# Two units at a time on the two row halves of the matrix array, in a two-MLP kernel on one core

## The chip, the cores and the metric

The kernel runs on one core of a Trainium2 chip. The metric is the device time of one execution in microseconds (us). TensorE (PE) multiplies matrices; VectorE (DVE), ScalarE (ACT) and GpSimd (POOL) work element by element; SyncE (SP) issues most of the transfers. A matmul multiplies a stationary operand (the weights, up to 128 rows by 128 columns) by a moving one (here 512 columns) and adds into one of eight PSUM banks, each of which holds 128 x 512 numbers in fp32. The rows of the array are the contraction dimension.

## The reference

```
x = softmax-weighted causal convolution of the input over 7 taps, 8 heads
                                     # [8192, 192]
h = x @ w_in1;   g = maximum(0.01*h, h);                      x = g @ w_out1
h = x @ w_in2;   g = h if h >= 1, 0 if h <= -1, else (h+1)^2/4;  out = g @ w_out2
                                     # w_in [192, 2048], w_out [2048, 192], all fp32
```

## The kernel before

The 8192 tokens are cut into 16 blocks of T = 512 (index j), the 2048 hidden channels into 16 slices of 128 (index f). One **unit** is (m, j, f): MLP m, block j, slice f. There are 512 of them. A unit has an up product (x of the block times one slice of w_in, into a bank h), a gate on ACT, DVE and POOL, and a down product (gate times one slice of w_out, added to the accumulators of the block).

To keep fp32 accuracy every operand is split in two numbers of type fp32r, a high part and a low part, and a product is high x high, high x low and low x high. x has 192 channels: 128 (part 0) and 64 (part 1). In part 1 the 64 channels lie twice in the 128 rows of the tile, and the weights `wi_b` hold the high part in one half and the low part in the other, so that all three products of part 1 take two matmuls. An up product is thus 3 + 2 = 5 matmuls of 128 rows x 512 columns (lines L584). The down product is 5 matmuls as well (L593): three for the output channels 0 to 127, and two for the channels 128 to 191, where `wo_b` holds high and low part side by side. So there are 10 matmuls to a unit and 5120 in all.

The gate of MLP 1 (m = 0) is two ACT activations (`gh`, and h itself) and one DVE subtraction (`gl`). The gate of MLP 2 (m = 1) is a DVE clamp (`s`), an ACT square, a DVE maximum (`g`), an ACT cast (`gh`) and a POOL subtraction (`gl`).

The order of all instructions comes from a planner (`Plan`) in the kernel: each step has an engine, a cost in ns and the steps that it depends on, and steps with a due time are put in order by how late they may be. The chip then runs each engine's list in that order. The first three blocks of MLP 1 run interleaved (`OFF`, `N0`), while the weights are loaded and split. After that units of MLP 1 and of MLP 2 alternate, and each MLP has two accumulator banks of its own (`acc_banks`): 4 and 5, and 6 and 7. The first three blocks also have their convolution done in part on PE (lines L529 and L534, plain fp32 matmuls, which need two passes); for the others DVE does all taps (L523).

Of the kernel before, what the change touches and what calls it, by code (L numbers as in the profile page):

```python
# [145 lines left out]
def kernel(  # L146
# [34 lines left out]
    PASS = 233  # L181
    UNIT = 10 * PASS
    LAG = 4

    HEAD = 0

    OFF = (0, 2, 4)
    N0 = len(OFF)

    E0 = 3  # L190

    CONV_BANKS = ((2, 3, 4), (5, 7, 6), (6, 7, 6))
# [4 lines left out]
    GO = 8  # L197
# [30 lines left out]
    wi_h = [cp.tile([128, NF, 128], F32R, name=f"wi_h{m}") for m in range(2)]  # L228
    wi_l = [cp.tile([128, NF, 128], F32R, name=f"wi_l{m}") for m in range(2)]
    wi_b = [cp.tile([128, NF, 128], F32R, name=f"wi_b{m}") for m in range(2)]  # L230
# [5 lines left out]
    def add_weights(t, m, o, g):  # L236
# [7 lines left out]
        def load():  # L244
# [7 lines left out]
            else:  # L252
                w = (w_in1, w_in2)[m].bitcast(U32)
                c = g * 512
                nc.sync.dma_start(out=t[:, 0:256].rearrange("p n t -> p (n t)"), in_=w[0:128, c:c + 512])  # L255
                for e in range(2):
                    nc.sync.dma_start(  # L257
                        out=t[DB * e:DB * (e + 1), 256:CW].rearrange("p n t -> p (n t)"),
                        in_=w[128:D, c + 256 * e:c + 256 * (e + 1)],
                    )  # L260
# [41 lines left out]
        if o == 0:  # L302
            part_a = lambda: ba()[:, 0:256].rearrange("p (k c) -> p k c", k=2)
            copy(400, wi_h[m][:, k, :], part_a)
            for e in range(2):
                r = slice(DB * e, DB * (e + 1))
                copy(300, wi_b[m][r, 2 * g + e], lambda r=r: ba()[r, 256:CW], 1)
            sub(pool, 930, wi_l[m][:, k, :], part_a, wi_h[m][:, k, :])
            for e in range(2):
                r = slice(DB * e, DB * (e + 1))  # L310
                q = slice(DB * (1 - e), DB * (2 - e))
                sub(pool, 450, wi_b[m][q, 2 * g + e], lambda r=r: ba()[r, 256:CW], wi_b[m][r, 2 * g + e], 1)
# [98 lines left out]
    xT, x1, x2 = {}, {}, {}  # L411

    spare = buf("x2", -4, [128, 4, T], F32R)
# [4 lines left out]
    def add_split(y, dst, part, lo_on=dve):  # L418

        hi, lo = 2 * part, 2 * part + 1  # L420
# [8 lines left out]

    def add_conv(at, j):  # L430
# [7 lines left out]
        dst = x1[j] = buf("x1" if j >= 2 else "x2", at, [128, 4, T], F32R)  # L438
# [98 lines left out]
        for i in range(2):  # L537
# [27 lines left out]
            add_split(y, dst, i, pool if (j, i) in LO_POOL else dve)  # L565


    acc = {}

    def add_unit(t, u):  # L570
        m, j, f = u
        src = (x1, x2)[m][j]
        h = bank(h_bank(t), t)
        a, b = buf("gh", t, [128, T], F32R), buf("gl", t, [128, T], F32R)
        first, last = f == 0, f == NF - 1
        if first:
            acc[m, j] = [bank(i, t) for i in acc_banks(m, j)]
        p = acc[m, j]

        def up(part):  # L580
            v = src()
            wh, wl, wb = wi_h[m][:, f], wi_l[m][:, f], wi_b[m][:, f]
            for i, (w, k) in enumerate(((wb, 2), (wb, 3)) if part else ((wh, 0), (wh, 1), (wl, 0))):
                nc.tensor.matmul(  # L584
                    out=h(), lhsT=w, rhs=v[:, k], start=(part == 0 and i == 0), stop=(part == 1 and i == 1)
                )

        def down(part):
            wh, wl = wo_h[m][:, f], wo_l[m][:, f]
            wb = wo_b[m][:, f].rearrange("p a d -> p (a d)")  # L590
            todo = ((wb, a), (wb, b)) if part else ((wh, a), (wl, a), (wh, b))
            for i, (w, v) in enumerate(todo):
                nc.tensor.matmul(  # L593
                    out=p[part](), lhsT=w, rhs=v(), start=(first and i == 0), stop=(last and i == len(todo) - 1)
                )

        key = ("w", m, 0, f // 2)
        for part in range(2):
            plan.add(
                pe, (2 if part else 3) * PASS, lambda part=part: up(part), reads=[(src, 2 * part), (src, 2 * part + 1), (key, part)],  # L600
                writes=[h, (h, part)] + (["under way"] if t == GO else []), uses=[src], due=UNIT * t - (HEAD if t == 0 else 0), chain=(h, "up"),
            )
        if m == 0:

            for dst in (a, h):
                plan.add(
                    act, 590,
                    lambda dst=dst: nc.scalar.activation(out=dst(), in_=h(), func=ACTF.Prelu, alpha=0.01),  # L608
                    reads=[h], writes=[dst], uses=[h],
                )  # L610
            plan.add(
                dve, 680, lambda: nc.vector.tensor_tensor(out=b(), in0=h(), in1=a(), op=ALU.subtract),  # L612
                reads=[h, a], writes=[b],
            )
        else:

            g, s = buf("g", t, [128, T]), buf("s", t, [128, T])
            plan.add(
                dve, 680, lambda: nc.vector.tensor_scalar(s(), h(), 1.0, -1.0, ALU.min, ALU.max),  # L619
                reads=[h], writes=[s],  # L620
            )
            plan.add(
# [185 lines left out]
```

## Time and profile before

| | |
|---|---|
| median of 3 executions | 1194.58 us (1194.23 to 1195.46) |
| span of the profiled execution, first to last instruction | 1192.7 us |
| busy in it: PE, PE weight load | 1186.8 us, 972.7 us |
| busy in it: DVE, ACT, POOL | 782.7 us, 734.3 us, 438.2 us |
| mean granted clock of PE, share of full speed | 0.999 |

The profile gives the span of the profiled execution; its own device time is not listed beside it, and the median of the three timed executions lies 1.9 us above the span. "Busy" of PE is the time in which at least one matmul is under way. Matmuls overlap, so that many more can fit into the same busy time; what counts is the time from the start of one to the start of the next.

### The profile page before, as it was taken

What the parts mean: (1) busy time and instruction counts of PE and PEld (TensorE: products, weight loads), DVE (VectorE), ACT (ScalarE), POOL (GpSimd) and SP (SyncE); (2) the same over time, 40 slices, a digit from 0 to 9 for tenths busy, and PEclk for the clock granted to TensorE, in tenths of its full rate; (3) what the DMA queues carried; (4) which work ended last, traced back from release to release, by engine and by line L of the source; (5) the groups of instructions that cost most, each with busy time, mean ns of one, the idle gap of its engine ahead of it and who ended that gap; (6) DMA issues with size and microseconds to landing.
All of it is one profiled execution on the core that took longest, in us unless ns stands there. A gap on an engine that the chain in (4) does not pass through costs nothing.

```text
span 1192.7 us, 15464 instructions
## 1 busy us (share of the span) xinstructions
PE 1186.8 (100%) x5210; PEld 972.7 (82%) x5210; DVE 782.7 (66%) x1209; ACT 734.3 (62%) x1296; POOL 438.2 (37%) x407
## 2 busy tenths in 40 slices
PE   9999999999999999999999999999999999999998
PEld 5788888888888888888888888888888888888887
DVE  7899897748567494764847658485674545447664
ACT  6777866656565565655656566565655656556654
POOL 4566374323223232232323233232233222335554
PEclk9999999999999999999999999999999999999999
DMA  4443111101001010010101001010000000000000
GB/s 132 117 104 99 43 43 18 23 1 23 10 9 23 1 23 9 15 18 1 32 1 23 10 10 23 1 23 1 1 14 1 14 1 3 12 1 14 14 14 14
DMA packets 114000, 27.90 MB, mean 23 GB/s; under 512 B 103680, under 2 KB 111872, under 8 KB 113920
## 3 DMA queue, kind: packets, MB, share of 16 engines
q1 hardware_dynamic: 113504, 26.69, 10.3%
q8 instruction: 40, 0.66, 0.2%
q14 instruction: 40, 0.33, 0.1%
q10 hardware_dynamic: 416, 0.23, 0.1%
HBM read 20.61 MB, written 6.29 MB: 23 GB/s over the span
## 4 chain that ended last, share of the span: by engine, by line
PE 99%; DMA 0%; SPq 0%; DVE 0%; issue 0%; ACT 0%; ACTq 0%
PE bank L584 49%; PE bank L593 49%; PE bank L529 1%; DMA wraw<-in_x_dram 0%; PE bank L534 0%; PE bank L328 0%; PE bank L478 0%; SPq L257 0%; PE bank L697 0%; SPq L255 0%; DVE s L714 0%; SPq L469 0%; DVE s L723 0%; ACT s L723 0%; ACTq L723 0%
## 5 line engine op out<-in xcount | busy, mean ns | idle before, releaser
L632 POOL TENSOR_TENSOR gl<-g,gh 128x512 fp32r<-128x512 f32 x256 | 343.2, 1343 | 677.6 <-ACT gh L630 674.7
L619 DVE TENSOR_SCALAR s<-bank 128x512 f32<-128x512 f32 x256 | 176.3, 689 | 303.4 <-PE bank L584 302.2
L584 PE MATMUL bank<-x,wi_h 128*128 128x512 f32 x1024 | 317.5, 391 | 0.0
L584 PE MATMUL bank<-x,wi_b 128*128 128x512 f32 x1024 | 316.9, 391 | 0.0
L623 ACT ACTIVATE s<-s,half 128x512 f32<-128x512 f32 x256 | 184.8, 722 | 192.7 <-DVE s L619 191.4
L630 ACT CAST gh<-g 128x512 fp32r<-128x512 f32 x256 | 158.6, 620 | 180.8 <-DVE g L627 178.1
L584 PEld LDWEIGHTS bank<-x,wi_h 128*128 128x128 f32 x1024 | 191.9, 188 | 42.2 <-issue 1.7
L584 PEld LDWEIGHTS bank<-x,wi_b 128*128 128x128 f32 x1024 | 192.2, 188 | 41.4 <-issue 1.4
L627 DVE TENSOR_TENSOR g<-bank,s 128x512 f32<-128x512 f32 x256 | 175.5, 686 | 67.8 <-ACT s L623 67.7
L593 PE MATMUL bank<-gh,wo_b 128*128 128x512 f32 x512 | 199.3, 389 | 0.0
L593 PE MATMUL bank<-gh,wo_h 128*128 128x512 f32 x512 | 199.3, 389 | 0.0
L593 PE MATMUL bank<-gl,wo_h 128*128 128x512 f32 x512 | 199.2, 389 | 0.0
L584 PE MATMUL bank<-x,wi_l 128*128 128x512 f32 x512 | 199.2, 389 | 0.0
L593 PE MATMUL bank<-gl,wo_b 128*128 128x512 f32 x512 | 199.2, 389 | 0.0
L593 PE MATMUL bank<-gh,wo_l 128*128 128x512 f32 x512 | 199.2, 389 | 0.0
L608 ACT ACTIVATE gh<-bank 128x512 fp32r<-128x512 f32 x256 | 152.8, 597 | 46.8 <-PE bank L593 25.3
L612 DVE TENSOR_TENSOR gl<-bank,gh 128x512 fp32r<-128x512 f32 x256 | 174.2, 680 | 9.8 <-ACT bank L608 9.2
L608 ACT ACTIVATE bank<-bank 128x512 f32<-128x512 f32 x256 | 151.8, 593 | 0.0
L523 DVE SCALAR_TENSOR_TENSOR xy<-xT,taps,xy 128x512 f32<-128x512 f32 x159 | 136.0, 878 | 0.2
L593 PEld LDWEIGHTS bank<-gl,wo_h 128*128 128x128 f32 x512 | 96.1, 188 | 20.0
L593 PEld LDWEIGHTS bank<-gh,wo_b 128*128 128x128 f32 x512 | 96.1, 188 | 20.0
L593 PEld LDWEIGHTS bank<-gh,wo_h 128*128 128x128 f32 x512 | 96.1, 188 | 20.0
(93 smaller groups left out, 741.5 us busy)
## 6 DMA issues: line engine op xcount, KB each, us to landing
xy<-in_x_dram SPq DMA_DIRECT2D x104, 64.0 KB, 2.4
wraw<-in_moe_w_out_dram SPq DMA_DIRECT2D x16, 384.0 KB, 3.0
out_dram<-o SPq DMA_DIRECT2D x90, 64.0 KB, 1.9
wraw<-in_moe_w_in_dram SPq DMA_DIRECT2D x16, 256.0 KB, 2.7
wraw<-in_moe_w_in_dram SPq DMA_DIRECT2D x32, 64.0 KB, 2.6
wraw<-in_x_dram SPq DMA_DIRECT2D x3, 384.0 KB, 5.3
out_dram<-s SPq DMA_DIRECT2D x1, 192.0 KB, 2.0
out_dram<-s ACTq DMA_DIRECT2D x1, 192.0 KB, 2.0
```

The costliest lines, as they stand in the source:

```text
L523: nc.vector.scalar_tensor_tensor(out=ys[i](), in0=t()[:, i, k:k + T], scalar=taps[:, i, k:k + 1], in1=ys[i](), op0=ALU.mult, op1=ALU.add,)
L529: nc.tensor.matmul(out=ys[1](), lhsT=flat(k), rhs=t()[:, 1, 2 * k:2 * k + T], start=(k == 0), stop=(k == NP - 1))
L584: nc.tensor.matmul(out=h(), lhsT=w, rhs=v[:, k], start=(part == 0 and i == 0), stop=(part == 1 and i == 1))
L593: nc.tensor.matmul(out=p[part](), lhsT=w, rhs=v(), start=(first and i == 0), stop=(last and i == len(todo) - 1))
L608: lambda dst=dst: nc.scalar.activation(out=dst(), in_=h(), func=ACTF.Prelu, alpha=0.01),
L612: dve, 680, lambda: nc.vector.tensor_tensor(out=b(), in0=h(), in1=a(), op=ALU.subtract),
L619: dve, 680, lambda: nc.vector.tensor_scalar(s(), h(), 1.0, -1.0, ALU.min, ALU.max),
L623: act, 720, lambda: nc.scalar.activation(out=s(), in_=s(), func=ACTF.Square, scale=0.5, bias=half),
L627: dve, 680, lambda: nc.vector.tensor_tensor(out=g(), in0=h(), in1=s(), op=ALU.max),
L630: plan.add(act, 620, lambda: nc.scalar.copy(a(), g()), reads=[g], writes=[a])
L632: pool, 1390, lambda: nc.gpsimd.tensor_tensor(out=b(), in0=g(), in1=a(), op=ALU.subtract),
```

## The change

Units are taken in **pairs** (m, j, p), slices 2p and 2p+1. In the up product the array is split into its upper and lower 64 rows. Slice 2p runs on rows 0 to 63 and slice 2p+1 on rows 64 to 127, each into a bank of its own. The 192 channels are three chunks of 64. The halves of x part 0 hold chunk 0 and chunk 1 (kept straight); a crossed copy of x holds chunk 1 and chunk 0 (made by DMA, or for the first block by ACT and DVE); part 1 holds chunk 2 twice. Each of the three steps has three products on both halves, so an up pair is 9 pairs of half-height matmuls. The weights of w_in are loaded in the layout that this needs, and `wi_b` is gone.

The down products of the first two blocks stay full height, 10 matmuls to a pair of units (L675 of the changed kernel). All later ones run on the halves too: each of the 10 matmuls becomes two with 64 rows, of which the lower half adds into a second set of accumulators. A chain of down products now owns four banks (4 to 7), and both MLPs share them, so one chain (m, j) runs at a time: all 8 pairs of a block, then the next block. At its end `gather` adds the two sets (an ACT copy and a DVE addition, twice). Two blocks instead of three are interleaved at the start. The order of PE's main products is now one fixed list (`steps`, chain "main"): the up product of pair n+2, then the down product of pair n.

```diff
-    OFF = (0, 2, 4)
-    E0 = 3
+    E0 = 2
-    COUNT = dict(wraw=4, wf=2, wa=2, wp=2, xy=4, xT=2, x1=2, x2=3, yz=2, g=2, s=2, gh=4, gl=4, o=1)
+    COUNT = dict(wraw=4, wf=2, wa=2, wp=2, xy=4, xT=2, x=3, yz=3, g=2, s=2, gh=4, gl=4, o=1)
...
+    def half_rows(outs, todo, start, stop):
+        for i, (w, v) in enumerate(todo):
+            for e, out_ in enumerate(outs):
+                r = slice(DB * e, DB * (e + 1))
+                nc.tensor.matmul(
+                    out=out_(), lhsT=w[e][r], rhs=v[e][r], start=start and i == 0, stop=stop and i == len(todo) - 1
+                )
...
+        def up(c):
+            v = src()
+            cols = [slice(128 * k, 128 * (k + 1)) for k in ((0, 1), (1, 0), (2, 2))[c]]
+            wh, wl = ([w[m][:, p, q] for q in cols] for w in (wi_h, wi_l))
+            hi, lo = ([v[:, 2 * c + i]] * 2 for i in range(2))
+            half_rows(hs, ((wh, hi), (wh, lo), (wl, hi)), c == 0, c == 1)
...
+            if full:
+                for i, (w, v) in enumerate(todo):
+                    nc.tensor.matmul(
+                        out=out_[part](), lhsT=w, rhs=v, start=start and i == 0, stop=stop and i == len(todo) - 1
+                    )
+            else:
+                half_rows(out_[part::2], [([w] * 2, [v] * 2) for w, v in todo], start, stop)
...
+    def gather(t, p, part):
+        z = buf("yz", t, [128, T])
+        plan.add(act, 590, lambda: nc.scalar.copy(z(), p[part]()), reads=[p[part]], writes=[z])
+        plan.add(
+            dve, 690, lambda: nc.vector.tensor_tensor(out=z(), in0=p[part + 2](), in1=z(), op=ALU.add),
+            reads=[p[part + 2], z], writes=[z],
+        )
+        return z
...
+    chains = [(0, 2), (1, 0), (1, 1)]
+    for j in range(3, NB):
+        chains += [(0, j), (1, j - 1)]
+    chains.append((1, NB - 1))
...
+    steps = ["U0", "U1", "D0"]
+    for n in range(2, EARLY, 2):
+        steps += [f"U{n}", f"U{n + 1}", f"D{n - 1}", f"D{n}"]
+    steps += [f"U{EARLY}", f"U{EARLY + 1}", f"D{EARLY - 1}"]
+    for n in range(EARLY, len(pairs)):
+        steps += [f"U{n + 2}"] * (n + 2 < len(pairs)) + [f"D{n}"]
```

On PE, in the middle of the program, one unit of MLP 2 stands so before (5 up matmuls, 5 down matmuls; `x2` means two with the same operands' names):

```order
L584 MATMUL bank1_65<-x2_3970,wi_h1_83 128x512 x2
L584 MATMUL bank1_65<-x2_3970,wi_l1_85 128x512
L584 MATMUL bank1_65<-x2_3970,wi_b1_87 128x512 x2
L593 MATMUL bank7_71<-gh_5235,wo_b1_93 128x512
L593 MATMUL bank7_71<-gl_5236,wo_b1_93 128x512
L593 MATMUL bank6_70<-gh_5235,wo_h1_89 128x512
L593 MATMUL bank6_70<-gh_5235,wo_l1_91 128x512
L593 MATMUL bank6_70<-gl_5236,wo_h1_89 128x512
```

In the changed kernel every row is a matmul on one half, and the rows come in twos. Here are the last two rows of an up pair and the first half of the down pair behind it, also in the middle of the program:

```order
L590 MATMUL bank0_64<-x_3561,wi_l0_84 128x512
L590 MATMUL bank1_65<-x_3561,wi_l0_84 128x512
L590 MATMUL bank5_69<-gh_4424,wo_b1_91 128x512
L590 MATMUL bank7_71<-gh_4424,wo_b1_91 128x512
L590 MATMUL bank5_69<-gl_4425,wo_b1_91 128x512
L590 MATMUL bank7_71<-gl_4425,wo_b1_91 128x512
L590 MATMUL bank4_68<-gh_4424,wo_h1_87 128x512
L590 MATMUL bank6_70<-gh_4424,wo_h1_87 128x512
L590 MATMUL bank4_68<-gh_4424,wo_l1_89 128x512
L590 MATMUL bank6_70<-gh_4424,wo_l1_89 128x512
L590 MATMUL bank4_68<-gl_4425,wo_h1_87 128x512
L590 MATMUL bank6_70<-gl_4425,wo_h1_87 128x512
```

So 10 rows of a down product take the place of 5, two by two on different halves and banks; counted over the program, PE has 9408 half-height rows and 160 full-height main rows in place of 5120.

Near the start of the changed kernel's program PE goes from half-height (L590) to a full-height convolution tap (L537) and full-height down products (L675), and back:

```order
L590 MATMUL bank3_67<-x_120,wi_l0_84 128x512
L537 MATMUL bank6_70<-xT_117,x_116 128x512
L675 MATMUL bank5_69<-gh_122,wo_b0_90 128x512
L675 MATMUL bank5_69<-gl_125,wo_b0_90 128x512
L675 MATMUL bank4_68<-gh_122,wo_h0_86 128x512
L675 MATMUL bank4_68<-gh_122,wo_l0_88 128x512
L675 MATMUL bank4_68<-gl_125,wo_h0_86 128x512
L675 MATMUL bank5_69<-gh_124,wo_b0_90 128x512
L675 MATMUL bank5_69<-gl_126,wo_b0_90 128x512
L675 MATMUL bank4_68<-gh_124,wo_h0_86 128x512
L675 MATMUL bank4_68<-gh_124,wo_l0_88 128x512
L675 MATMUL bank4_68<-gl_126,wo_h0_86 128x512
```

Before, PE used the array at full height throughout; now it changes between the two 24 times, all but the last of them while the first two blocks run.

On DVE at the end of a chain of MLP 2, the changed kernel has the two additions of `gather` (L696) behind the gate of the next chain's first pair (L630) and three convolution taps (L531) of a later block:

```order
L630 TENSOR_TENSOR gl_4552<-bank0_64,gh_4550 128x512
L630 TENSOR_TENSOR gl_4570<-bank1_65,gh_4569 128x512
L531 SCALAR_TENSOR_TENSOR xy_4531<-xT_3027,taps_73,xy_4531 128x512
L531 SCALAR_TENSOR_TENSOR xy_4504<-xT_3027,taps_73,xy_4504 128x512
L531 SCALAR_TENSOR_TENSOR xy_4531<-xT_3027,taps_73,xy_4531 128x512
L696 TENSOR_TENSOR yz_4270<-bank7_71,yz_4270 128x512
L696 TENSOR_TENSOR yz_4209<-bank6_70,yz_4209 128x512
```

Before there was no such addition, and the first down product of a chain waited for the accumulators of its own MLP only.

## Rows read from the trace of the kernel before

**Rows 1.** The page's first part: busy us, share of span, instructions.

```profile
PE 1186.8 (100%) x5210; PEld 972.7 (82%) x5210; DVE 782.7 (66%) x1209; ACT 734.3 (62%) x1296; POOL 438.2 (37%) x407
```

**Rows 2.** The waits of PE: all that the view lists.

```profile
PE bank L328 <- POOL own L340: 1.1, 1, 1.1
PE bank L478 <- DMA wraw<-in_x_dram: 1.1, 2, 0.8
```

**Rows 3.** PE groups: line, operands, count | busy us, mean ns | idle before.

```profile
L584 PE MATMUL bank<-x,wi_h 128*128 128x512 f32 x1024 | 317.5, 391 | 0.0
L584 PE MATMUL bank<-x,wi_b 128*128 128x512 f32 x1024 | 316.9, 391 | 0.0
L584 PE MATMUL bank<-x,wi_l 128*128 128x512 f32 x512 | 199.2, 389 | 0.0
L593 PE MATMUL bank<-gh,wo_b 128*128 128x512 f32 x512 | 199.3, 389 | 0.0
L593 PEld LDWEIGHTS bank<-gh,wo_b 128*128 128x128 f32 x512 | 96.1, 188 | 20.0
```

**Rows 4.** Timeline in steady state: start us, length us, engine, line.

```profile
600.12 0.62 PE L584 MATMUL bank<-x,wi_h 128*128 128x512 f32 x2
601.03 0.19 PEld L593 LDWEIGHTS bank<-gh,wo_b 128*128 128x128 f32 x1
604.66 0.61 PE L584 MATMUL bank<-x,wi_h 128*128 128x512 f32 x2
...
1180.39 0.62 PE L584 MATMUL bank<-x,wi_h 128*128 128x512 f32 x2
```

**Rows 5.** Timeline of the tail.

```profile
1186.98 0.39 PE L593 MATMUL bank<-gl,wo_h 128*128 128x512 f32 x1
1187.36 0.97 PEld L697 LDWEIGHTS bank<-same,yz 128*128 128x128 f32 x8 [0.41 <-ACT yz L691]
1187.36 1.10 PE L697 MATMUL bank<-same,yz 128*128 128x64 f32 x8
1188.30 0.61 PE L706 MATMUL bank<-ident,xy 128*128 128x128 f32 x4
```

**Rows 6.** Timeline of the start, PE only.

```profile
13.09 2.73 PE L529 MATMUL bank<-xT,x 128*128 128x512 f32 x6
17.26 0.39 PE L328 MATMUL bank<-zero 128*128 128x512 bf16 x1
18.10 1.47 PE L328 MATMUL bank<-zero 128*128 128x512 bf16 x6
```

**Rows 7.** Groups of DVE, ACT and POOL: count | busy us, mean ns | idle before.

```profile
L619 DVE TENSOR_SCALAR s<-bank 128x512 f32<-128x512 f32 x256 | 176.3, 689 | 303.4 <-PE bank L584 302.2
L612 DVE TENSOR_TENSOR gl<-bank,gh 128x512 fp32r<-128x512 f32 x256 | 174.2, 680 | 9.8 <-ACT bank L608 9.2
L523 DVE SCALAR_TENSOR_TENSOR xy<-xT,taps,xy 128x512 f32<-128x512 f32 x159 | 136.0, 878 | 0.2
L272 DVE SCALAR_TENSOR_TENSOR wf<-wraw,wf 128x384 uint32<-128x384 uint32 x32 | 20.8, 649 | 0.8
L278 DVE TENSOR_SCALAR wp<-wraw 128x384 uint32<-128x384 uint32 x32 | 17.7, 565 | 0.0
L269 DVE TENSOR_SCALAR wf<-wa 128x384 uint32<-128x384 uint32 x32 | 13.4, 420 | 2.4 <-ACT wa L265 2.3
L623 ACT ACTIVATE s<-s,half 128x512 f32<-128x512 f32 x256 | 184.8, 722 | 192.7 <-DVE s L619 191.4
L630 ACT CAST gh<-g 128x512 fp32r<-128x512 f32 x256 | 158.6, 620 | 180.8 <-DVE g L627 178.1 <-PE bank L593 1.7 <-PE bank L584 0.9
L647 ACT COPY yz<-bank 64x512 f32<-64x512 f32 x16 | 9.3, 584 | 7.4 <-PE bank L593 7.3
L632 POOL TENSOR_TENSOR gl<-g,gh 128x512 fp32r<-128x512 f32 x256 | 343.2, 1343 | 677.6 <-ACT gh L630 674.7
```

**Rows 8.** Stretch 50 to 100 us: busy us (count) of PE, PEld, DVE, ACT, POOL; clock; DMA.

```profile
50.00:100.00 50.00, 50.00 (x222) 41.39 (x222) 47.37 (x78) 40.35 (x89) 31.14 (x39) 1.00 0.43 112
```

More of the change, by code (lines that the diff above doesn't have):

```diff
@@ L302, in add_weights @@
         if o == 0:
[L303 to L312, printed above, removed]
+            copy(550, wi_h[m][:, g], ba)
+            sub(pool, 1280, wi_l[m][:, g], ba, wi_h[m][:, g])
         else:
@@ L565, in add_conv @@
             add_split(y, dst, i, pool if (j, i) in LO_POOL else dve)
[L568 to L575, printed above, removed]
-        if first:
[L577 to L588, printed above, removed]
+            if i == 0:
+                add_cross(dst, None if j else y)
@@ L589, in down, with add_down @@
+    def add_down(n):
+        m, j, p = pairs[n]
+        full = n < EARLY
+        first, last = p == 0, p == NF // 2 - 1
+        if first:
+            acc[m, j] = [bank(i, 2 * n) for i in ((4 + 2 * j, 5 + 2 * j) if full else (4, 5, 6, 7))]
+        out_ = acc[m, j]
+        def down(e, part):
+            a, b = gates[n][e]
+            f = 2 * p + e
             wh, wl = wo_h[m][:, f], wo_l[m][:, f]
             wb = wo_b[m][:, f].rearrange("p a d -> p (a d)")
-            todo = ((wb, a), (wb, b)) if part else ((wh, a), (wl, a), (wh, b))
@@ L592, in down @@
-            for i, (w, v) in enumerate(todo):
-                nc.tensor.matmul(
-                    out=p[part](), lhsT=w, rhs=v(), start=(first and i == 0), stop=(last and i == len(todo) - 1)
-                )
[L597 to L602, printed above, removed]
@@ new lines, in down @@
+            start, stop = first and e == 0, last and e == 1
+            if full:
+                for i, (w, v) in enumerate(todo):
+                    nc.tensor.matmul(
+                        out=out_[part](), lhsT=w, rhs=v, start=start and i == 0, stop=stop and i == len(todo) - 1
+                    )
+            else:
+                half_rows(out_[part::2], [([w] * 2, [v] * 2) for w, v in todo], start, stop)
+        for e in range(2):
+            for part in (1, 0):
+                cost = (2 if part else 3) * PASS
+                plan.add(
+                    pe, cost, lambda e=e, part=part: down(e, part), reads=[*gates[n][e], (("w", m, 1, p), part)],
+                    writes=out_[part::2], due=main(cost), chain="main",
+                )
@@ L649, in finish1 @@
         plan.add(
-            dve, 690, lambda: nc.vector.tensor_tensor(out=y(), in0=p[1](), in1=z(), op=ALU.add),
-            reads=[p[1], z], writes=[y],
-        )
-        add_split(p[0], dst, 0)
-        add_split(y, dst, 1)
+            dve, 690, lambda: nc.vector.tensor_tensor(out=z(), in0=pb(), in1=z(), op=ALU.add),
+            reads=[pb, z], writes=[z],
+        )
+        add_split(pa, dst, 0)
+        add_cross(dst)
+        add_split(z, dst, 1)
     def finish2(t, j, p):
-        z, y = buf("yz", t, [128, T]), buf("yz", t, [128, T])
+        ya, yb = (gather(t, p, i) for i in (0, 1))
@@ L765 @@
         seen = set()
-        for t, (m, j, f) in enumerate(units):
-            if m == 0 and f == 0:
-                add_conv(t - AHEAD, j)
-            for o in range(2):
-                if (m, o, f // 2) not in seen:
-                    seen.add((m, o, f // 2))
-                    add_weights(t, m, o, f // 2)
-            add_unit(t, (m, j, f))
+        for step in steps:
+            up, n = step[0] == "U", int(step[1:])
+            m, j, p = pairs[n]
+            if up and m == p == 0:
+                add_conv(2 * n - AHEAD, j)
+            o = int(not up)
+            if (m, o, p) not in seen:
+                seen.add((m, o, p))
+                add_weights(2 * n + o, m, o, p)
+            (add_up if up else add_down)(n)
         for tag, count in COUNT.items():
```

229 lines of the change are left out of this document (129 added, 100 removed).

## The prediction

> **What bounds the kernel now.** First the page's busy times: PE is busy for the whole span, DVE for 66%, ACT for 62% [rows 1]. A busy PE need not be a PE that is fed, so the next view is its waits: there are 2.2 us in all, on the warm-up (L328) and on the transposes of the first blocks' input (L478), both in the head [rows 2], and the clock was granted in full, which is the 2.4 GHz level: 1.00 in the stretch from 50 to 100 us [rows 8]. The groups then give the count: up products 1024 + 1024 + 512 = 2560, down products 5 x 512 = 2560, together 5120 matmuls of 128 rows by 512 columns [rows 3]. Their recorded 390 ns overlap; the price of one is the time from start to start. Twenty starts lie between 600.12 and 604.66 us, 0.227 us each. To sharpen that: from 600.12 to 1180.39 us, both the first matmul of a unit, 580.27 us hold 2560 starts (256 units of ten), so one costs **0.2267 us** [rows 4]. 5120 x 0.2267 = 1160.5 us of the 1192.7 us. Of the other 32.2 us, the tail from the last main product (1186.98 + 0.23) to the end is 5.5 us [rows 5], and 26.7 us are the head: warm-up, convolution taps and waiting before the stream is dense. So between head and tail the kernel is a queue of matmuls with no hole, and only their number and price count.
>
> **The number of passes.** A pair of units took 20 matmuls. Now its up product is 9 pairs of half-height matmuls and its down product 10 pairs (10 full ones in the first two blocks). If two halves cost together what one full matmul costs, 256 x 19 = 4864 passes remain: 4864 x 0.2267 = **1102.5 us**, 58.0 us less. Everything rests on the price of two halves, which no row shows, since before never uses part of the rows. The bounds:
> - From below: two weight loads are needed per pass now. In the tail eight loads of 128 x 128 take 0.97 us with 0.19 us for one, so they follow each other after (0.97 - 0.19) / 7 = 0.111 us, although one is recorded with 0.19 us [rows 5]. Two in turn are 0.222 us, and a pass cannot be cheaper if they go one by one: 4864 x 0.222 = 1080 us.
> - From above: the halves run one after the other, 0.453 us.
> - The rows in between: the same 512 columns in bf16 follow each other after (1.47 - 0.39) / 5 = 0.216 us [rows 6]. So an fp32r matmul has 0.011 us over its columns; if each half pays that singly, a pass is 0.2377 us.
>
> I take 0.2267 us: the two loads (0.222) just fit under it, and in steady state a load already starts 0.23 us ahead of its matmul, during the one before [rows 4], so loading under a running matmul is what the chip does here. It is a close fit: every nanosecond per pass is 4.9 us, and at about 10 ns the gain is gone.
>
> The Trainium skill, "TensorE: Matmul & The Clock Gate", Part 3 (Measured speedup vs the span model), has tiles in different row groups starting some 4 ns apart, so a pass of two would be 0.231 us and my sum 20 us more. No row here bears on that, and the sum does without it.
>
> **Changing the height.** 24 times PE goes between half and full height. The nearest row is PE starting afresh in the tail: 0.38 us from start to start, 0.15 more than in the stream [rows 5]. The most it could cost is that a matmul runs out (0.389) and the next load (0.188) lies open: 0.35 more [rows 3]. I take 0.2 each, near the row that shows a restart: **4.8 us**, from 0 to 8.4. "TensorEngine Tiling (Array Packing)" of the Trainium skill, Tiling Modes, Key Properties, says that a change of the tiling mode drains the array; it gives no figure, and the row of a restart is the price for it.
>
> **The head.** One block fewer has its convolution on PE: eight passes of taps, each (2.73 - 0.59) / 5 = 0.43 us where 0.59 is one record's length [rows 6], and eight transposes at about the 0.11 us of the tail's products [rows 5]: 4.3 us less, if PE's work is what fills the head. Against it the first block's crossed copy puts two ACT copies of 64 rows (0.58) and two DVE subtractions (about 0.65) ahead of the first unit's last step [rows 7], 2.5 us. So the head lies between 22.4 and 29.2 us; I take **25**.
>
> **The tail.** The last block's transposes now add two sets. Four more products of 64 columns, recorded in two passes each, at 0.11 us, and eight products of 128 columns in two passes where four transposes stood, twelve more at 0.11: 2.2 us [rows 5]. After the last up product only two down pairs (4.5 us) cover the gate of the last pair, which is clamp, square, maximum and cast (0.69 + 0.72 + 0.69 + 0.62) and two POOL subtractions in turn (1.34 each), 5.4 us for its second unit, which is asked for 1.6 us into its down product: next to nothing is open, 0.3 us. Tail: 5.5 + 2.5 = **8 us**.
>
> **The ends of chains.** There are 29 places where one chain must leave banks 4 to 7 before the next enters. Banks 5 and 7 are done 3 passes before the end of the last down product and wanted after the up product behind it, 3 + 9 passes = 2.7 us; banks 4 and 6 have 9 + 2 passes = 2.5 us. The work is two ACT copies (0.58 each, priced by the copy of 64 rows) and two DVE additions (0.68 each, as the subtraction that reads a bank) [rows 7]: the first addition ends at about 1.3 us, the second at 2.0 us after the banks of the first are done. That leaves 1.4 us at the first and 1.2 us at the second, which counts from its own banks. What stands ahead of it on DVE is gate work that is 0.68 us per piece and taps of 0.88 us; two pieces begun too late eat the cover. I cost it at nothing; if the cover fails, every 0.1 us is 2.9 us, up to some 10 us.
>
> **The gates in steady state** are covered: between the end of an up product and the down product that needs its gates lie two down and two up products, 38 passes = 8.6 us, for 5.4 us of gate. In a round of one chain of each MLP (16 pairs, 68.9 us) DVE has 8 x 4 x 0.69 + 8 x 2 x 0.68 + 13.4 for one block's convolution (12 taps of 0.878 and four smaller pieces) + 7.2 at the two ends = 53.5 us, 78%. Before, DVE was at 66%. The early part is tighter. Up to the chain of block 3, 40 pairs or 172 us, DVE has the splitting of all weights, 32 x (0.649 + 0.565 + 0.420) = 52.3 us, gates of 24 pairs at 1.36 and 16 at 2.75 = 76.6, two convolutions 26.7 and finishing work 12: 167.6, of which some 6 fall into the head, so 94% [rows 7]. Between 50 and 100 us before, DVE was at 95% and PE lost nothing [rows 8], but then PE came to new weight slices every 13.6 us (six units) and now does every 8.6 us (two pairs). I add **3 us**, from 0 to 15. The crossed copies of later blocks are DMAs between buffers in SBUF, two per block and MLP. They stand behind loads on SP's queue, but have a chain's length (8 pairs, 34 us) until PE wants them; I cost them at nothing.
>
> **The sum:** 1102.5 + 25 + 4.8 + 3 + 8 = 1143.3 us of span. The median of the runs stood 1.9 us above the profiled span, so **1145 us**, 4.1% less than 1194.58. With the smaller terms at their ends (head -2.6 to +4.2, height -4.8 to +3.6, gates -3 to +12, chain ends 0 to +10) the likeliest case spans 1130 to 1165 us.
>
> **The rivals.**
> - *Another engine holds PE back.* DVE in the first 200 us, or the chain ends, cost tens of us where I have 3. For it: DVE at 94% there with a planner that counts a tap with 0.78 us where the row shows 0.88 [rows 7]. Against: stage 50 to 100. 20 to 45 us more: 1165 to 1190.
> - *The halves each pay the fixed part.* A pass is 0.2377 us: 4864 x 0.2377 = 1156.2 + 40.8 + 1.9 = 1199, next to no change. For it: the fp32r price has that part, and two loads at 0.222 leave only 2% of room. Against: in the tail a matmul and a load together follow each other at 0.11 us, so four instructions per pass need no more than 0.224.
> - *A weight load of one half lies open in every pass* (the one that ends on the other side). The mechanism: a half's next weights are held until the pair is done. Price 0.111 per pass: 0.338 x 4864 = 1643 + 43 = 1686 us. It decides from 0.010 us per pass on. Against: at full height loads run ahead [rows 4]; but no row shows it for halves. The page on TensorE of the Trainium skill, same part, measured 3.07 instead of 4 for four row tiles; by that share of 77% a pass would be an estimated 0.295 us and the time 1478.
> - *The halves don't overlap at all.* 9408 + 160 = 9568 matmuls at 0.2267 = 2169 + 43 = 2212 us. Against it only that the two write different banks and read different rows; no row of before can exclude it.
>
> **Chances.** Forecast 0.60; another engine 0.10; fixed part twice 0.12, with its time spread over some 1170 to 1240, a quarter of it faster; an open load or a part of one 0.08; no overlap 0.10. The range 1125 to 1240 holds the first three, 0.82, less a little at its ends; 1125 is two loads as the bound (1080 + 40.8 + 1.9 = 1123). Faster by over 0.2%, about what a measurement of this kernel can tell from no change: 0.60 + 0.10 + 0.03 = 0.73; within: 0.03; slower: 0.24.
>
> **What would show it.** Right: in steady state two matmuls of line 590 start per 0.227 us, the list of waits of PE stays short outside the first 200 us, and ten pairs of a down product take 2.27 us. The price of a pass is read there directly, and each of the rivals on the halves has its own (0.238, 0.338, 0.453). The chain ends show as waits of PE on DVE's additions at line 696; the early part as waits on L630 or on weights; a change of height as a longer distance from start to start at L590 next to L675. The forecast fails first if the distance in steady state is over 0.237 us, and next if PE's idle time sums to more than 50 us.

## The result, and the profile after

The changed kernel takes **1156.12 us** (median; 1155.72 to 1157.5), 0.968 of the time before (95% interval 0.9667 to 0.9694), 38 us less. The forecast was 1145 us, faster. The direction and the price of a pass were right; 11 us that the forecast had gained are missing, and most of this part is about them. (One correction to the text ahead, which has everything in fp32: the weights arrive as 64-bit numbers, two 32-bit words each. That is why each pair of slices, here called a weight slice, goes through several steps, `wa`, `wf`, `wp`, `wa` again and the high and low parts, on ACT, DVE, DVE, POOL, and ACT with POOL.)

The page after, busy times and three groups (busy us, mean ns | idle before); they answer to [rows 1, 3]:

```profile
PE 1137.4 (99%) x9662; PEld 1081.5 (94%) x9662; DVE 865.3 (75%) x1278; ACT 752.1 (65%) x1320; POOL 421.6 (37%) x375
...
L590 PE MATMUL bank<-x,wi_h 64*128 64x512 f32 x3072 | 533.5, 388 | 4.1 <-ACT wi_h L285 2.7
...
L590 PEld LDWEIGHTS bank<-x,wi_h 64*128 64x128 f32 x3072 | 403.5, 184 | 21.2 <-issue 4.1
...
L590 PE MATMUL bank<-gh,wo_b 64*128 64x512 f32 x960 | 249.5, 388 | 1.9 <-POOL wo_b L290 1.9
```

One half-height matmul is recorded with 388 ns and its load with 184, as the full ones were; there are nearly twice as many, and weight loading is now seen for 94% of the span. What a pass costs stands in the timeline of the steady state (the first and the last rows of one down product, and the next up product's first):

```profile
601.31 0.56 PE L590 MATMUL bank<-gh,wo_b 64*128 64x512 f32 x2
601.54 0.56 PE L590 MATMUL bank<-gl,wo_b 64*128 64x512 f32 x2
...
603.35 0.56 PE L590 MATMUL bank<-gl,wo_h 64*128 64x512 f32 x2
603.58 0.39 PE L590 MATMUL bank<-x,wi_h 64*128 64x512 f32 x1
```

Ten passes of two halves in 603.58 - 601.31 = 2.27 us: 0.227 us each, exactly what one full matmul cost [rows 4]. 4864 of them are 1102.5 us.

A change of height in the first stage (L590 works on halves, L675 on the full array), and the tail:

```profile
34.02 0.39 PE L590 MATMUL bank<-x,wi_l 64*128 64x512 f32 x2
34.34 0.50 PE L675 MATMUL bank<-gh,wo_b 128*128 128x512 f32 x1
34.68 0.40 PE L675 MATMUL bank<-gl,wo_b 128*128 128x512 f32 x1
...
1146.51 0.49 PE L590 MATMUL bank<-gl,wo_h 64*128 64x512 f32 x2
1146.93 2.00 PE L763 MATMUL bank<-same,yz 128*128 128x64 f32 x16
1148.77 2.00 PE L763 MATMUL bank<-ident,xy 128*128 128x128 f32 x16
```

From 34.02 to 34.68 two distances take 0.66 us where two passes take 0.45: a change costs 0.2 us, spread over two distances; 24 are 4.8 us. From the last main pass (its second half starts at 1146.6; 0.23 more) to the end of the span at 1154.8 are 8.0 us.

So the span of 1154.8 us has 1102.5 for passes, 8.0 for the tail, 4.8 for the height, and 39.5 for all else, against 25 + 3 in the forecast. Where the difference lies, the stretches from 150 us show (length; then busy us and instructions of PE, PEld, DVE, ACT, POOL; granted clock; DMA):

```profile
150.00:160.00 10.00, 6.30 (x50) 4.21 (x46) 9.59 (x16) 5.01 (x11) 7.85 (x8) 1.00 0.35 94
160.00:170.00 10.00, 7.47 (x46) 5.19 (x48) 7.86 (x11) 6.06 (x11) 8.82 (x9) 0.83 0.00 1
170.00:180.00 10.00, 9.92 (x86) 7.70 (x82) 9.11 (x14) 7.63 (x16) 8.58 (x9) 1.00 0.33 71
180.00:190.00 10.00, 8.16 (x58) 6.74 (x60) 10.00 (x15) 7.13 (x12) 8.22 (x7) 0.83 0.23 36
190.00:200.00 10.00, 10.00 (x92) 8.56 (x90) 8.84 (x16) 5.96 (x10) 5.61 (x5) 1.00 0.24 41
```

A dense stretch holds 92 halves, these four hold 50, 46, 86 and 58: 128 halves too few, 64 passes x 0.2267 = 14.5 us. A stretch also counts matmuls that run across its edges, so this is a little too much: by starts alone there are 238 from 149 to 190 us where 362 have room, a loss of **14.0 us**. The waits of PE in that time are 8.1 of them (total, times, longest):

```profile
PE bank L590 <- ACT wi_h L285: 2.7, 2, 2.0
PE bank L590 <- POOL wi_l L290: 2.1, 2, 1.5
PE bank L590 <- POOL wo_b L290: 1.9, 1, 1.9
PE bank L590 <- DVE g L647: 1.4, 1, 1.4
```

Part of the rest is the clock after the waits. In two of the stretches its mean is 0.83, and the timeline there has pass starts 0.43 us apart, then 0.23 again. Two narrower stretches have it at 0.50:

```profile
161.50:164.80 3.30, 3.30 (x18) 2.39 (x16) 2.53 (x3) 1.15 (x3) 2.78 (x3) 0.50 0.00 0
182.00:185.30 3.30, 3.30 (x16) 2.61 (x18) 3.30 (x6) 1.48 (x3) 3.30 (x3) 0.50 0.25 39
...
162.22 0.64 PE L590 MATMUL bank<-x,wi_l 64*128 64x512 f32 x2
162.65 0.63 PE L590 MATMUL bank<-gh,wo_b 64*128 64x512 f32 x2
163.08 0.70 PE L590 MATMUL bank<-gl,wo_b 64*128 64x512 f32 x2
...
165.10 0.40 PE L590 MATMUL bank<-gl,wo_b 64*128 64x512 f32 x2
165.33 0.40 PE L590 MATMUL bank<-gh,wo_h 64*128 64x512 f32 x2
```

That is the lower level, 1.2 GHz. The first of the two stretches comes after pauses of PE of 1.4, 2.0 and 0.6 us that end at 152.4, 159.0 and 160.4 us, the second after one of 1.9 us that ends at 181.8 us. In each of them nine distances from pass to pass take 1.7 us more than at the full clock, 3.4 us together. Some 2.5 us are left over. About 1.5 of them are the restarts after six pauses: the last pass before a pause is recorded with 0.39 us where a pass in the stream takes 0.227, and the second pass after it comes 0.33 us behind the first (152.38 and 152.72 us).

Three of the four waits are for pieces of weights. The first gate step of MLP 2, its clamp, shows when PE reaches MLP 2 and how fast it then goes through it (count: ns; first and last start), in the changed kernel from 100 to 170 us and in the kernel before from 100 to 250 us:

```profile
L638 DVE TENSOR_SCALAR s<-bank x14: 675/679/692, 130.9 to 166.8; 128x512 f32<-128x512 f32 x14
L619 DVE TENSOR_SCALAR s<-bank x26: 652/690/692, 135.0 to 247.9; 128x512 f32<-128x512 f32 x26
```

PE comes to MLP 2 at about 130 us, 4 us sooner than before. The larger difference is the rate. Before, units of the two MLPs alternated: one unit of MLP 2 every (247.9 - 135.0) / 25 = 4.5 us, and new weights for two units every 9. Now one chain runs at a time, and PE asks for the weights of a pair every 19 passes = 4.3 us. Up to 149 us it finds them ready and loses nothing; then they come late. Why?

### The profile page after: what moved, and what is told of

Its sections match the earlier page's. It is cut to its first block, busy times and chain, and to the rows that moved or that the text cites. A ratio compares the mean times of both kernels' runs of the same rounds, so it can differ in the third digit from the quotient of the medians.

```text
span 1154.8 us, 24741 instructions
## 1 busy us (share of the span) xinstructions
PE 1137.4 (99%) x9662; PEld 1081.5 (94%) x9662; DVE 865.3 (75%) x1278; ACT 752.1 (65%) x1320; POOL 421.6 (37%) x375
## 4 chain that ended last, share of the span: by engine, by line
PE 95%; DVE 2%; issue 1%; ACT 1%; POOL 1%; DMA 1%; SPq 0%; ACTq 0%; DVEq 0%; POOLq 0%
PE bank L590 90%; PE bank L675 3%; PE bank L537 1%; DMA wraw<-in_x_dram 1%; DVE g L647 0%; DVE wf L261 0%; DVE s L638 0%; PE bank L763 0%; ACT s L643 0%; POOL wa L274 0%; DVE wp L270 0%; PE bank L542 0%; POOL gl L653 0%; PE bank L312 0%; ACT wa L257 0%
## 5 line engine op out<-in xcount | busy, mean ns | idle before, releaser
L590 PE MATMUL bank<-x,wi_h 64*128 64x512 f32 x3072 | 533.5, 388 | 4.1 <-ACT wi_h L285 2.7
L590 PEld LDWEIGHTS bank<-x,wi_h 64*128 64x128 f32 x3072 | 403.5, 184 | 21.2 <-issue 4.1
L590 PE MATMUL bank<-x,wi_l 64*128 64x512 f32 x1536 | 392.7, 387 | 2.1 <-POOL wi_l L290 2.1
L625 ACT ACTIVATE gh<-bank 128x512 fp32r<-128x512 f32 x246 | 146.4, 599 | 199.2 <-PE bank L590 194.4
L630 DVE TENSOR_TENSOR gl<-bank,gh 128x512 fp32r<-128x512 f32 x246 | 165.1, 681 | 147.8 <-PE bank L590 111.3
L590 PE MATMUL bank<-gh,wo_b 64*128 64x512 f32 x960 | 249.5, 388 | 1.9 <-POOL wo_b L290 1.9
L590 PE MATMUL bank<-gl,wo_b 64*128 64x512 f32 x960 | 249.5, 388 | 0.0
L590 PE MATMUL bank<-gh,wo_h 64*128 64x512 f32 x960 | 249.2, 387 | 0.0
L590 PE MATMUL bank<-gh,wo_l 64*128 64x512 f32 x960 | 249.0, 387 | 0.0
L590 PE MATMUL bank<-gl,wo_h 64*128 64x512 f32 x960 | 249.0, 387 | 0.0
L590 PEld LDWEIGHTS bank<-x,wi_l 64*128 64x128 f32 x1536 | 236.5, 184 | 8.5 <-POOL wi_l L290 3.0
L590 PEld LDWEIGHTS bank<-gh,wo_b 64*128 64x128 f32 x960 | 152.1, 185 | 4.6 <-POOL wo_b L290 2.3
L590 PEld LDWEIGHTS bank<-gl,wo_b 64*128 64x128 f32 x960 | 151.7, 185 | 3.0 <-POOL gl L653 0.8
L590 PEld LDWEIGHTS bank<-gh,wo_h 64*128 64x128 f32 x960 | 152.0, 185 | 2.2
L590 PEld LDWEIGHTS bank<-gh,wo_l 64*128 64x128 f32 x960 | 151.9, 185 | 2.3
L590 PEld LDWEIGHTS bank<-gl,wo_h 64*128 64x128 f32 x960 | 151.8, 185 | 2.3
L531 DVE SCALAR_TENSOR_TENSOR xy<-xT,taps,xy 128x512 f32<-128x512 f32 x171 | 150.6, 911 | 0.6
```

The source lines that it names most:

```text
L531: nc.vector.scalar_tensor_tensor(out=ys[i](), in0=t()[:, i, k:k + T], scalar=taps[:, i, k:k + 1], in1=ys[i](), op0=ALU.mult, op1=ALU.add,)
L590: nc.tensor.matmul(out=out_(), lhsT=w[e][r], rhs=v[e][r], start=start and i == 0, stop=stop and i == len(todo) - 1)
L625: lambda dst=dst, h=h: nc.scalar.activation(out=dst(), in_=h(), func=ACTF.Prelu, alpha=0.01),
L630: lambda a=a, b=b, h=h: nc.vector.tensor_tensor(out=b(), in0=h(), in1=a(), op=ALU.subtract),
```

## The experiments

Times in brackets are ratios to the kernel before with their 95% interval.

**Is it DVE's time?** Two tries on the forecast's own suspicion that DVE is full. The first moves one step of MLP 2's slices to POOL, the second tells the planner what DVE's steps take beside POOL.

```diff
 e1_rest_pool
-            nc.vector.tensor_scalar(bp(), raw()[:, :, 0], 2.0 ** -29, None, ALU.mult)
+            engine[pool if m else dve].tensor_scalar(bp(), raw()[:, :, 0], 2.0 ** -29, None, ALU.mult)
 e2_costs
-        plan.add(dve, 430, rest, reads=[raw], writes=[bp])
+        plan.add(dve, 800, rest, reads=[raw], writes=[bp])
-            lo_on, 710 if lo_on == dve else 1500,
+            lo_on, 1050 if lo_on == dve else 1500,
-                        dve, 780, lambda i=i, k=k: tap(i, k), reads=[(t, i), y], writes=[y], uses=[t],
+                        dve, 900, lambda i=i, k=k: tap(i, k), reads=[(t, i), y], writes=[y], uses=[t],
```

> The changed kernel, but the DVE step of splitting MLP 2's weights that makes wp (16 instructions, 0.35 us alone and up to 1.2 us beside POOL) runs on POOL. Theory (DVE is the bound between 100 and 190 us, and PE's 14 us of lost time there are DVE work that comes late): DVE has 8 to 16 us less to do there, so PE loses under 6 us between 149 and 190 us and the time is 1142 to 1150 us against 1156. Rival 1 (the chain of steps for one weight slice is long, no matter which engine): 14 us stay lost, 1155 to 1158 us. Rival 2 (POOL, 66% busy there, is the bound): PE waits longer on POOL's rows, 1160 us or more.

> The changed kernel, but the planner counts three kinds of DVE steps with what they took beside POOL: taps 900 instead of 780 ns, wp 800 instead of 430, the low part of a split of x 1050 instead of 710. Nothing else differs than the order. Theory (DVE has too much to do for any order): the loss between 149 and 190 us stays within 4 us of 14, so 1152 to 1160 us. Rival (the order is at fault, work for the later block is done ahead of MLP 2's weights because it is counted too cheap): the loss falls by more than 6 us, under 1150 us.

Measured: 1158.45 us (0.97, 0.9685 to 0.9714) and 1157.27 us (0.9686, 0.9671 to 0.97). Neither helps: the theory of the first fell, and so did the rival of the second. With the step on POOL, DVE falls to 7 of 10 us in the first 20 us of the stage, POOL is nearly full, and PE loses as much (the stretches of `e1_rest_pool`):

```profile
150.00:160.00 10.00, 5.69 (x42) 4.02 (x42) 7.11 (x11) 5.53 (x12) 8.91 (x9) 0.88 0.15 42
160.00:170.00 10.00, 9.13 (x60) 6.70 (x58) 6.87 (x10) 5.14 (x9) 9.75 (x10) 0.78 0.00 1
```

DVE with time to spare and PE still waiting: DVE alone is not the cause. POOL's extra work clouds this run; what follows is cleaner.

**What do height and the order of the halves cost?**

```diff
 e3_down_full: all down products at full height, two banks per chain
-        full = n < EARLY
+        full, turn = True, n // (NF // 2) % 2
...
 e4_halves_apart
-        for i, (w, v) in enumerate(todo):
-            for e, out_ in enumerate(outs):
+        for e, out_ in enumerate(outs):
+            for i, (w, v) in enumerate(todo):
```

> The changed kernel with all down products at full height (two accumulator banks to a chain, no gather): 4864 passes as before, but PE changes its height 498 times instead of 24. Theory (a change of height costs 0.2 us wherever it stands): 474 x 0.2 = 95 us more, less some 2 us in the tail and up to 12 us of waiting that a slower PE no longer sees: 1235 to 1250 us. Rival (in a dense stream the change is hidden, and half-height down products bring nothing): 1140 to 1156 us.

> The changed kernel with the same matmuls in another order inside each step: the three (or two) products of the upper half first, then those of the lower half, instead of in turn. Theory (PE starts matmuls strictly in their order, so halves overlap only where they stand next to each other): a step of three takes 2 x (2 x 0.227 + 0.05) = 1.01 us instead of 0.68, one of two 0.56 instead of 0.45, in all 1562 us of passes and about 1605 us. Rival 1 (PE looks ahead and starts a later matmul of the free half): 1156 us. Rival 2 (no overlap at all in this order): about 2210 us.

`e3_down_full`: 1258.57 us (1.0542, 1.0521 to 1.0563), slower than before. That is above the 1235 to 1250 us expected. 474 more changes of height cost 102.4 us, 0.216 each, a little more than the forecast's 0.2, and the 102.4 are net: PE waits 5.2 us for gates and weights in this kernel and 9.8 in the changed one. In that kernel's stretch of 200 us in steady state 1174 matmuls start:

```profile
600.00:800.00 200.00, 200.00 (x1174) 142.67 (x1174) 121.90 (x181) 109.97 (x190) 47.38 (x40) 1.00 0.13 25
```

A pair of units has 18 + 10 = 28, so it takes 4.77 us instead of 4.31: two changes for 0.46, 0.23 each. With the down products left at full height the change would have lost.

`e4_halves_apart`: 1156.28 us (0.968), the same. The theory that PE starts matmuls strictly in the program's order fell. The timeline of this kernel:

```profile
600.51 0.39 PE L590 MATMUL bank<-gh,wo_b 64*128 64x512 f32 x1
600.60 0.39 PE L590 MATMUL bank<-x,wi_h 64*128 64x512 f32 x1
600.73 0.39 PE L590 MATMUL bank<-gl,wo_b 64*128 64x512 f32 x1
600.82 0.39 PE L590 MATMUL bank<-x,wi_l 64*128 64x512 f32 x1
600.96 0.39 PE L590 MATMUL bank<-gh,wo_h 64*128 64x512 f32 x1
601.05 0.39 PE L590 MATMUL bank<-gh,wo_b 64*128 64x512 f32 x1
```

Two streams are to be seen, each with 0.22 us from start to start: one is already in the down product (600.51, 600.73, 600.96) while the other finishes the up product (600.60, 600.82) and follows at 601.05. In the program the `gh,wo_b` of both halves stand ahead of this `gh,wo_h`; in the trace one half starts its `gh,wo_h` (600.96) before the other starts its `gh,wo_b` (601.05).

**Do the loads of the two halves go one by one?** Every half-height matmul becomes two of 256 columns, with twice the loads.

```diff
 e5_two_cuts
-                nc.tensor.matmul(
-                    out=out_(), lhsT=w[e][r], rhs=v[e][r], start=start and i == 0, stop=stop and i == len(todo) - 1
-                )
+            for n in range(2):
+                for e, out_ in enumerate(outs):
+                    r, c = slice(DB * e, DB * (e + 1)), slice(256 * n, 256 * (n + 1))
+                    nc.tensor.matmul(
+                        out=out_()[:, c], lhsT=w[e][r], rhs=v[e][r][:, c], start=start and i == 0 and n == 0,
+                        stop=stop and i == len(todo) - 1 and n == 1,
+                    )
```

> Every half-height product is issued as two products of 256 columns, so the weight loads double and the streamed columns stay. Theory (the two halves are two streams of their own, and a load on one half goes under a product of the other or of its own half): a pass of two halves pays the fixed part of a product once more, 0.2267 + 0.0133 = 0.240 us, in 4704 passes 63 us: 1215 to 1225 us. Rival (weight loads of the two halves go one by one at 0.111 us): four loads in a pass, 0.444 us, about 2170 us. Between them lies a load that the next product of its own half must wait for (0.06 to 0.11 us a load not hidden): 1450 to 1700 us.

1216.18 us (1.0182, 1.0168 to 1.0196), as the two streams would have it: 60.1 us over 4704 passes, 0.0128 us each. The steady state of this kernel:

```profile
600.92 0.52 PE L594 MATMUL bank<-gh,wo_b 64*128 64x256 f32 x4
601.16 0.52 PE L594 MATMUL bank<-gl,wo_b 64*128 64x256 f32 x4
601.40 0.52 PE L594 MATMUL bank<-gh,wo_h 64*128 64x256 f32 x4
```

Four matmuls with four loads in 0.24 us. At 0.111 us one by one, the loads alone would take 0.444. So the loads of the two halves overlap, and the forecast's lower bound (two loads in turn, 0.222 us) was no bound; 0.2267 was not a close fit.

**Where do 14 us go: buffers, engines or demand?** A slice keeps one of two buffers `wa` from its scaling on ACT to its last subtraction on POOL. Theory A: this loop is too slow with two buffers. Theory B: the engines have no time.

```diff
 e6_in_place (frees wf; four wa, three wp)
-    COUNT = dict(wraw=4, wf=2, wa=2, wp=2, xy=4, xT=2, x=3, yz=3, g=2, s=2, gh=4, gl=4, o=1)
+    COUNT = dict(wraw=4, wa=4, wp=3, xy=4, xT=2, x=3, yz=3, g=2, s=2, gh=4, gl=4, o=1)
-            nc.vector.tensor_scalar(bf(), ba().bitcast(U32), 3, None, ALU.logical_shift_left)
+            nc.vector.tensor_scalar(ba().bitcast(U32), ba().bitcast(U32), 3, None, ALU.logical_shift_left)
...
 e7_no_taps
-                for k in range(1, KP if shared else K):
+                for k in range(1, 2 if j in (2, 3) else KP if shared else K):
 e8_weave (and full-height down products there)
+    woven = set()
+    for i in range(NP2 + 2):
+        for j, p in ((0, i), (1, i - 2)):
+            if 0 <= p < NP2:
+                woven.add(len(pairs))
+                pairs.append((1, j, p))
...
 e9_wa3 (one number, from the changed kernel)
-    COUNT = dict(wraw=4, wf=2, wa=2, wp=2, xy=4, xT=2, x=3, yz=3, g=2, s=2, gh=4, gl=4, o=1)
+    COUNT = dict(wraw=4, wf=2, wa=3, wp=2, xy=4, xT=2, x=3, yz=3, g=2, s=2, gh=4, gl=4, o=1)
 e10_in_place_two (control of e6_in_place)
-    COUNT = dict(wraw=4, wa=4, wp=3, xy=4, xT=2, x=3, yz=3, g=2, s=2, gh=4, gl=4, o=1)
+    COUNT = dict(wraw=4, wa=2, wp=2, xy=4, xT=2, x=3, yz=3, g=2, s=2, gh=4, gl=4, o=1)
```

> The splitting of a weight slice works in place, so that four slices instead of two can be under way in the first step and three instead of two in the others; the instructions on each engine stay the same in number and size. Theory A (the 14 us lost from 149 to 190 us come from a loop through ACT, DVE, POOL and back that has only two buffers): the loss falls by 6 us or more, 1144 to 1150 us. Theory B (the engines that split the weights haven't the time: DVE 94 of 100 us busy from 100 to 200 us, POOL 43 of 50 from 140 to 190): within 3 us of the changed kernel, 1153 to 1159 us.

> Leaves out all taps but the first two of the convolution of blocks 2 and 3 on DVE, so that these blocks come out otherwise; 10 to 12 us of DVE's work in the stretch from 85 to 190 us are gone, nothing is added elsewhere. Theory B (work on DVE ahead of the stage sets how many weight slices of the second MLP are ready): the loss from 149 to 190 us falls by 6 us or more, 1144 to 1150 us. Theory A (a loop of two buffers): the loop is as long as before, 1153 to 1158 us.

> Blocks 0 and 1 of the second MLP are woven, two weight slices for two pairs, as in the first MLP's first two blocks, with full-height down products there; so the weights of the second MLP are asked for at half the rate, every 8.6 us a pair of slices instead of every 4.3. Both theories of a supply of weights that is too slow (A and B): the loss from 149 to 190 us falls from 14 to 1 to 4 us, and 32 more changes of height cost 32 x 0.2 = 6.4 us: 1149 to 1154 us. If weights are not what holds PE back there, only the price is left: 1161 to 1164 us.

> The changed kernel with three buffers wa instead of two, nothing else. If wa alone holds the loop (its buffer is kept from the scaling on ACT to the last subtraction on POOL), the loop of two slices in 9 us becomes one of three, and half or more of the 14 us lost from 149 to 190 us is gone: 1147 to 1151 us. If wf and wp hold it as much, or the instructions' own time in place does it: 1154 to 1158 us.

> The splitting in place as in the run of 1147.24 us, but with two buffers wa and two wp as in the changed kernel: the control of that run. If the buffers gave its 9 us: 1154 to 1159 us. If working in place did it by itself: 1146 to 1149 us.

| run | us | ratio, interval |
|---|---|---|
| e6_in_place, four wa | 1147.24 | 0.9605, 0.9592 to 0.9618 |
| e7_no_taps, two wa | 1154.10 | 0.9659, 0.9646 to 0.9672 |
| e8_weave, two wa | 1154.03 | 0.9669, 0.9656 to 0.9682 |
| **e9_wa3, three wa** | **1145.97** | **0.9594, 0.9581 to 0.9607** |
| e10_in_place_two, two wa | 1158.51 | 0.97, 0.9686 to 0.9713 |

One more buffer of 1.5 KB per partition takes 10.2 us off, more than the 1147 to 1151 us expected. The control with two buffers has all of the loss again, so working in place is not what did it. Less work on DVE (e7) brought 2.0 us, far from B's 6. Asking at half the rate (e8) ended the waits for weights in that stage; it gained 2.1 us after paying an estimated 32 x 0.2 = 6.4 us for the height, at the edge of what was expected, because one wait of 1.6 us for `g` and a slow clock after it (0.83 from 190 to 200 us) remain.

The stretches of `e9_wa3`:

```profile
150.00:160.00 10.00, 9.67 (x84) 7.49 (x82) 10.00 (x15) 6.79 (x13) 8.93 (x9) 1.00 0.22 55
160.00:170.00 10.00, 10.00 (x90) 8.20 (x90) 10.00 (x15) 7.61 (x14) 8.70 (x8) 1.00 0.01 2
170.00:180.00 10.00, 9.23 (x79) 7.24 (x77) 9.92 (x16) 7.88 (x13) 7.67 (x7) 1.00 0.71 131
180.00:190.00 10.00, 10.00 (x89) 8.62 (x88) 9.41 (x15) 5.75 (x9) 6.00 (x5) 1.00 0.08 15
```

Counted in the same way, 26 halves are missing instead of 128, 2.9 us instead of 14.5, and the clock stays at 1.00. And all waits of PE in that run, none of them on weights:

```profile
PE bank L486 <- DMA wraw<-in_x_dram: 2.7, 2, 1.6
PE bank L312 <- POOL own L324: 1.1, 1, 1.1
PE bank L590 <- POOL gl L653: 0.8, 1, 0.8
PE bank L590 <- DVE g L647: 0.3, 1, 0.3
PE bank L590 <- DVE gl L630: 0.2, 1, 0.2
```

DVE is fuller than in the changed kernel (39 of 40 us, there 37), which speaks against B by itself. The loop is read from the scaling step of the slices after 100 us (count: ns; first and last start), first of the changed kernel:

```profile
L257 ACT ACTIVATE wa<-wraw x13: 529/543/554, 108.6 to 174.4; 128x384 f32<-128x384 f32 x13
```

of e9_wa3:

```profile
L257 ACT ACTIVATE wa<-wraw x11: 532/550/564, 107.2 to 146.4; 128x384 f32<-128x384 f32 x11
```

and of e6_in_place:

```profile
L257 ACT ACTIVATE wa<-wraw x9: 533/550/557, 111.4 to 135.1; 128x384 f32<-128x384 f32 x9
```

A slice starts every (174.4 - 108.6) / 12 = 5.5 us with two buffers, every 39.2 / 10 = 3.9 with three, every 23.7 / 8 = 3.0 with four. Times the buffers that is 11.0, 11.8 and 11.8 us from one use of a buffer to its next, on average; single slices hold theirs for shorter and longer. The steps on one slice take some 4 to 5 us by themselves (the sum of their records), so most of this is waiting between them. A pair of units needs one slice of `w_in` and one of `w_out`, so PE asks for a slice every 2.15 us once it is in MLP 2, and without a loss it would come to the last pair at an estimated 160 us. With three buffers the scaling of the last slice begins at 146.4 us, ahead of that, with two at 174.4, behind it.

Two tries to take the rest from the in-place kernel:

```diff
 e11_in_place_costs: e6_in_place with the costs of e2_costs
 e12_in_place_pool: e6_in_place with
-            nc.vector.tensor_scalar(bp(), raw()[:, :, 0], 2.0 ** -29, None, ALU.mult)
+            engine[pool if m and g > 3 else dve].tensor_scalar(bp(), raw()[:, :, 0], 2.0 ** -29, None, ALU.mult)
```

> The splitting in place with four wa and three wp, and the planner's costs of DVE's steps raised to what they took beside POOL (wp 800, x 1050, taps 900 ns). What that run lost from 200 to 220 us (3.9 us: a wait of 1.5 us for gl on DVE behind four taps in a row, and the clock after it) should go if the order did it: 1142 to 1145 us. If DVE has no time to give before 205 us (99% busy from 150 to 210): 1146 to 1149 us.

> The splitting in place with four wa and three wp, and the step wp of the last four slice pairs of the second MLP on POOL instead of DVE (8 steps, about 7 us of DVE's time before 190 us). If DVE's time before 205 us is what the rest of the loss comes from: 1142 to 1145 us. If POOL, 10.0 of 10 us busy from 150 to 160 us, is then late: 1147 to 1152 us.

1147.11 us (0.9603, 0.9589 to 0.9616) and 1148.57 us (0.9616, 0.9603 to 0.963): no gain, and a loss of 1.3 us. The scaling steps of `e11_in_place_costs`, which has four buffers, are a warning:

```profile
L257 ACT ACTIVATE wa<-wraw x11: 533/542/565, 109.3 to 163.3; 128x384 f32<-128x384 f32 x11
```

One starts every 5.4 us, as slowly as with two buffers, and yet the loss of 14 us is not back. The last one still starts 11 us sooner than in the changed kernel, for 21 of the 32 slices were begun before 109 us, against 19. So the number of buffers decides whether the slices can be early enough; at which rate they then run is the order's doing too, and 11 to 12 us is no fixed time of a slice. The quickest kernel stays e9_wa3, 0.9% under the changed kernel.

## Why the forecast was right, and where it was off

- **Passes and their price: right.** 256 passes fewer at an unchanged 0.2267 us are the 58 us. All three rivals on the price (0.2377, 0.338, 0.453) fell in the steady state. The doubt that gave them 0.30 of the chances came in part from reading the 0.111 us between loads in the tail [rows 5] as the limit of one loading path; `e5_two_cuts` shows that the halves load side by side. The forecast's own price had two grounds. That loading goes on under a running matmul held; that two loads in turn just fit under 0.2267 us did not, and no row of before used part of the rows, so the right price was in part luck. The Trainium skill, "TensorE: Matmul & The Clock Gate", Part 3 (Measured speedup vs the span model), has tiles in different row groups start some 4 ns apart, and the estimate of 0.231 us that the forecast worked out from it does not hold here. A pass is 0.227 us with the halves 0.17 us apart (a pair is recorded with 0.56 us in the steady state, one half with 0.39), and it is no longer with the halves within 0.02 us of each other (a pair recorded with 0.40 at 165.10 and 165.33 us), so the offset is not paid in every pass.
- **Change of height: right**, 0.2 us by the timeline, 0.216 to 0.23 in `e3_down_full`. The Trainium skill, "TensorEngine Tiling (Array Packing)", Tiling Modes, Key Properties, states that a change of the mode drains the array; the trace agrees in that every change of height costs time, 0.2 us here.
- **Tail: right**, 8.0 us. **Ends of chains: right**, nothing: PE has no wait on line 696. It is close: some of the variants have one, of 0.2 to 1.2 us.
- **Head: right.** 39.5 - 14.0 = 25.5 us remain for the head and a wait of 1.7 us for `wo_b` at 37 us, so the head is some 24 (forecast 25, from 22.4 to 29.2).
- **The term "gates and early part", 3 us from 0 to 15: this failed.** It was 14.0 + 1.7 = 15.7 us, over its upper end. Its size was argued from DVE's load up to 172 us, and its place from the stretch of 50 to 100 us [rows 8], with a pair of slices every 8.6 us. The loss was at 150 to 190, where one chain at a time asks for a pair every 4.3 us, and the limit was not DVE's time but two buffers, each used again only every 11 us. The forecast compared the rates in the first MLP alone (13.6 us before, 8.6 after) and left out the second, where the rate doubles (9 us before, 4.3 after). Before, the same two buffers just did: its scaling steps ran until 183.1 us, later than now, and PE lost nothing there (the second line is one of its stretches):

```profile
L265 ACT ACTIVATE wa<-wraw x13: 534/540/556, 102.3 to 183.1; 128x384 f32<-128x384 f32 x13
...
170.00:180.00 10.00, 10.00 (x46) 8.29 (x45) 9.96 (x15) 6.38 (x15) 7.42 (x8) 1.00 0.01 2
```

PE now reaches the stage 4 us sooner (130.9 against 135.0 us) and goes through its weights twice as fast, so the lead that had covered the supply was used up by 149 us. By these rates the new order of the chains did more here than the smaller number of passes; `e8_weave`, which asks at half the rate, has no wait for weights in this stage. With `wa` at three the kernel takes 1145.97 us, where the forecast had 1145.
- **The rival "another engine holds PE back"** had the right place, the first 200 us, and the right sign, but it put 20 to 45 us over the forecast where 11 were measured, and no engine's time was the limit.

Given back from the 58 us, then, by the spans (1192.7 to 1154.8): the early part 15.7, height 4.8, tail 2.5, less 2.9 that the head won (26.7 to 23.8); 58.0 - 20.1 = 37.9.

Open: what the remaining 4 to 6 us from 150 to 220 us in the kernels with more buffers hang on (neither the planner's costs nor a step on POOL brought a shorter time), and whether four `wa` beside two `wf` and `wp` would do better, which no run shows.

## What to carry to other kernels

When a change makes the bound engine faster or gives it another order, look for every supply that was just in time, and compare its rate with the new rate of demand stage by stage, at its highest and not on the mean. A new order can do more to a demand than a faster engine: here it doubled one. For a supply through several engines, count the buffers: buffers divided by the mean time from one use to the next is its rate, and one number in a table can be worth more than moving work about. Two halves of the array are worth using where K is too short for a full one, if neighbouring products are split alike, since each change of height costs about a whole pass.

## What was not expected of the hardware

- The two row halves run as two streams, each at 0.2267 us per matmul of 512 columns, loads included; one may be ahead of the other and start matmuls that the program has behind the other's.
- A pause of PE costs more than itself: 8.1 us of waits came to a loss of 14.0 us. 3.4 us of the rest fell in two stretches at the 1.2 GHz level (granted clock 0.50), and about 1.5 us was restarting after the pauses.
